# Clustered attention with a gated feed-forward layer on one core: one split and four loads moved in the listed opening, and a planner with other banks, dates and constants

## The chip, the cores and the metric

The kernel runs on one core of a Trainium2 chip. The time is the device time of one execution in microseconds (us), as the median of several runs. The engines are PE (TensorE, matrix products), ACT (ScalarE), DVE (VectorE), POOL (GpSimd) and SP, which here only issues DMAs. POOL issues DMAs too.

## What is computed

For 4 batches and 8 heads, queries and keys (768 tokens of 64 numbers) are each assigned to the nearest of 16 centroids of their head. A query attends only to keys of its own cluster. The result, 3072 tokens of 512 numbers, goes through `w_in` (512 to 2048), a SiLU gate and `w_out` (2048 to 512).

```python
    q_assign = np.argmax(np.einsum('bhsd,hcd->bhsc', q_n, c_n), axis=-1)
    k_assign = np.argmax(np.einsum('bhsd,hcd->bhsc', k_n, c_n), axis=-1)
    mask = q_assign[:, :, :, None] == k_assign[:, :, None, :]
    scores = scale * np.matmul(q, k.transpose(0, 1, 3, 2))
    scores = np.where(mask, scores, -1000000000.0)
    ...
    attn = attn / (np.sum(attn, axis=-1, keepdims=True) + 1e-09)
    return np.matmul(attn, v).astype(np.float32)
...
    h = x @ w_in
    g = h * (1.0 / (1.0 + np.exp(-h)))
    return (g @ w_out).astype(np.float32)
```

## The kernel before

**The work of one head.** A job holds the rows of q and k of one head and batch. Jobs 0 to 7 are batch 0 (`k0` to `k7`, with three of six query blocks; `x0` and `x1` hold the other three blocks of four heads each); jobs 8 to 31 are batches 1 to 3. A job's steps are:

- `load` (line 111, SP): the raw rows come in, as two DMAs for jobs 8 to 31 (q, then k).
- `hi` and `lo`: the rows are split into two f16 halves, upper and lower. The upper half is made by ACT, DVE or POOL (lines 123, 127, 125), the lower always by DVE (line 132), which reads the upper half.
- The halves are transposed into the tile `ab`: in batch 0 by PE (`tr`, line 155) and a copy out of the bank (`ev`, lines 164 and 166), in batches 1 to 3 by a DMA transpose that SP issues (`xpose`, line 141).
- Logits against the centroids on PE (`psN`, line 180, twelve small products), sums, maximum and comparison on DVE (lines 192, 208, 217). The codes of the cluster go into spare rows of `ab`: by a product with the identity, a copy (`cd`, line 257 or 259) and a small DMA (line 261), or in batches 2 and 3 by a DMA transpose (line 233) and a move from POOL (line 237). Two heads of batch 0 (`ct`) have no DMA in this.

**Units.** A unit is one pair of score products (`pS`, line 354) and one exponential on ACT (`P`, line 359). There are 192, 24 for each half of a batch, three for each head and half. The score tiles have two buffers. After six units, `pv` (line 371, 36 small products) makes the output of two heads, DVE normalises it, and it is transposed into `xt`.

**Feed-forward.** When four such pairs are done, sixteen pieces `a` (`ph`, line 421, four products with `win_s`) each give a gate (tanh on ACT, line 441, and product on DVE, line 444). Pieces `b` multiply by `wout_s`: plain tiles `po` in four quarters of four products (line 480), or pairs with seven products out of differences (line 562). Quarter n needs the four `w_out` chunks of piece n.

**Weights.** `w_in` comes in eight pieces (`w0` to `w7`, line 618) and `w_out` in four (`w8` to `w11`, line 621), all issued by POOL, which also casts values (`v`, line 295) and makes some upper halves. Their queue is apart from SP's. `w10` and `w11` wait for exponentials 22 and 23 by a small copy (line 614).

**Order.** Two things set it. The opening is the list `plan`, one word for each step, which writes each engine's instructions in that order: `hi6.P` is the upper half of job 6 on POOL, `lo6` its lower half, `tr6.20` its transposes into banks 2 and 0, `ce2.A` the copy of job 2's codes on ACT with the DMA behind it, `r8` the load of job 8, `e7.0` the end of piece `a` number 7 in bank 0. It ends with the eight gates `e0 e1 e6 e4 e2 e3 e5 e7`. Everything behind is written by a planner that keeps a clock for each engine and picks at each step a piece that is ready by its own costs and due times. Its constants: `PACE` and the like date the scores; `SPLIT` gives the unit at which a job of batches 1 to 3 is split, and `AHEAD`, `VALUES` and `CAST` how many units before or after it its rows, values and cast are asked for; `ROOM` (one for each of batches 1 to 3) is added to the time at which a transpose is taken to land, before the job's logits may be placed on PE; `CODES` and `TURN` do the same for codes and for `xt`; `MARGIN` decides when ACT takes a copy from DVE.

**Banks.** PE's small results share four banks. A piece of the planner takes the first bank of the list `free`, sorted by `freed`, the planned time of release. Before the change the planner starts with `free` as 0, 1, 2, 3, all with time 0.

Of the kernel before, what the change touches and what calls it, by code (L numbers as in the profile page):

```python
# [34 lines left out]
def kernel(  # L35
# [753 lines left out]
    plan = """  # L789
        hk0 hq0 hi1.A lk0 cn0 lq0 lo1 tk0.0 hi2.A evk0.D j3.1 c5.12 kad tq0.3 lo2 evq0.A tr1.23 stk vl4 L0.0 vl0  # L790
        evq1.A evk1.D mx0 ge0 hi4.A tr2.13 evq2.A L1.2 hi3.P ct0.03 lo4 mx1 ge1 xr0 cm1 ctk0 hi5.P evk2.A lo5 ctq0
        tr4.10 ce1.A qk0 hi7.P evk4.A lo3 L2.3 evq4.A tr5.21 mx2 evk5.D ge2 qk1 ex0 qk2 evq5.A w0 lo7 L4.0 vl1 ex1 mx4
        cm2 tr3.12 ex2 ce2.A xr1 qk3 evq3.D evk3.A qk4 hi6.P tr7.32 ge4 lo6 cm4 L3.1 evq7.D xh0.P ex3 qk5 vl2 evk7.D
        ce4.A v4 mx3 w1 ex4 tr6.20 evk6.D ex5 L5.3 ge3 mx5 vl5 qk6 v1 evq6.A ct3.21 vl3 ge5 qk7 cm5 L6.0 xl0 ctk3 ex6
        ctq3 qk8 ce5.A L7.S.2 xq0.3 mx6 ge6 w2 ls7 xp0.1 xw0.D v0 xh1.P ex7 cm6 v2 v5 qk9 ex8 ce6.A qk10 ex9 pa0.3 mx7
        ge7 pb0 vl6 xu0.D xl1 qk11 xL0.0 ex10 cm7 vl7 qk12 v3 ex11 xM0 ce7.D xs0 w3 pc0 v7 qk13 r8 xp1.1 ex12 qk14 xm0
        ex13 xu1.D ex14 w4 xq1.2 qk15 xg0 v6 nm0 pa1.1 qk16 xw1.D xc0 pt0.3 ex15 xe0.D ex16 qk17 ex17 xL1.2 w5 pb1
        qk18 vl8 ex18 xM1 qk19 pe0.D pc1 qk20 nm1 vl9 xs1 pa2.0 ex19 ex20 qk21 pb2 qk22 ex21 pc2 xm1 xg1 ex22 nm2 w6
        qk23 px3.3 pt1.1 pe1.D ex23 pt2.0 xc1 py3 qk24 pe2.D w7 r9 xe1.A r10 nm3 ex24 qk25 a0.1 pt3.0 w8 qk26 a1.2
# [559 lines left out]
```

## Time and profile before

| what | value |
|---|---|
| median of 3 runs | 299.75 us (299.74 to 303.74) |
| the profiled execution | 301.13 us |
| its span, first to last instruction | 298.7 us |
| PE busy | 288.7 us (97%) |
| DVE, ACT, POOL busy | 224.2, 217.8, 71.1 us |
| PE's waits for other engines and DMAs, all eight kinds | 6.3 us |

A profile's time is counted from the span's start. A row of a timeline gives start, length, engine, line, what is written and read, how many, and in brackets the idle time before and what ended it. A row on DMAs of a line gives their count, how long the issue took, when the first and last were issued, and below it the time from issue to landing (least, median, most).

### The profile page before, as it was taken

What the parts mean: (1) busy time and instruction counts of PE and PEld (TensorE: products, weight loads), DVE (VectorE), ACT (ScalarE), POOL (GpSimd) and SP (SyncE); (2) the same over time, 40 slices, a digit from 0 to 9 for tenths busy, and PEclk for the clock granted to TensorE, in tenths of its full rate; (3) what the DMA queues carried; (4) which work ended last, traced back from release to release, by engine and by line L of the source; (5) the groups of instructions that cost most, each with busy time, mean ns of one, the idle gap of its engine ahead of it and who ended that gap; (6) DMA issues with size and microseconds to landing.
All of it is one profiled execution on the core that took longest, in us unless ns stands there. A gap on an engine that the chain in (4) does not pass through costs nothing.

```text
span 298.7 us, 8186 instructions
## 1 busy us (share of the span) xinstructions
PE 288.7 (97%) x3281; PEld 204.1 (68%) x3281; DVE 224.2 (75%) x470; ACT 217.8 (73%) x357; POOL 71.1 (24%) x133
## 2 busy tenths in 40 slices
PE   7889989799999999999999999999999999999995
PEld 3777756466676566668766876678767777776884
DVE  5989678468999869999788966988674644469653
ACT  4989879653996569996488668997798788844410
POOL 2995710010042003453432214423200000000000
PEclk9999999999999999999999999999999999999999
DMA  6888999979999598999998699786400020110014
GB/s 210 248 199 161 191 250 214 160 200 206 226 215 230 117 181 200 256 182 214 180 194 165 136 180 262 178 137 114 115 22 15 13 87 13 50 37 0 35 37 140
DMA packets 77365, 44.61 MB, mean 149 GB/s; under 512 B 56305, under 2 KB 73233, under 8 KB 77329
## 3 DMA queue, kind: packets, MB, share of 16 engines
q1 hardware_dynamic: 72096, 35.62, 54.2%
q0 software_dynamic: 4800, 8.13, 14.9%
q8 instruction: 25, 0.41, 0.6%
q10 hardware_dynamic: 432, 0.36, 0.4%
q14 instruction: 12, 0.09, 0.1%
HBM read 27.30 MB, written 6.29 MB: 112 GB/s over the span
## 4 chain that ended last, share of the span: by engine, by line
PE 78%; DMA 11%; DVE 3%; ACT 3%; issue 2%; POOL 1%; SPq 1%; POOLq 0%; ACTq 0%; DVEq 0%
PE ph L421 24%; PE po L562 17%; PE pS L354 16%; PE pO L371 10%; DMA wout_s<-in_moe_w_out_dram 8%; PE po L480 7%; PE psN L180 3%; ACT P L359 2%; DMA ab<-cd 2%; DMA raw<-in_q_dram 1%; POOL hl L125 1%; DVE hl L132 1%; DVE ab L166 1%; DVE mxn L208 1%; SPq L111 0%
## 5 line engine op out<-in xcount | busy, mean ns | idle before, releaser
L359 ACT ACTIVATE P<-pS 128x768 f16<-128x768 f32 x192 | 156.3, 823 | 37.2 <-PE pS L354 36.5
L421 PE MATMUL ph<-xt,win_s 128*128 128x384 f16 x512 | 97.9, 326 | 0.8 <-DVE gt L444 0.8
L354 PE MATMUL pS<-ab 128*128 128x384 f16 x384 | 93.0, 326 | 0.5 <-DMA ab<-cd 0.3
L444 DVE SCALAR_TENSOR_TENSOR gt<-tn,ph 128x384 f16<-128x384 f32 x112 | 60.6, 550 | 21.4 <-ACT tn L441 20.6
L421 PEld LDWEIGHTS <-win_s 128*128 128x128 f16 x512 | 49.1, 98 | 31.9 <-issue 1.1
L441 ACT ACTIVATE tn<-ph 128x384 f32<-128x384 f32 x112 | 56.2, 507 | 5.9 <-PE ph L421 4.9
L354 PEld LDWEIGHTS <-ab 128*128 128x128 f16 x384 | 34.5, 98 | 19.0 <-DMA ab<-cd 0.9
L371 PEld LDWEIGHTS <-P 128*128 128x128 f16 x1152 | 39.9, 97 | 4.5 <-DVE ab L166 0.2
L371 PE MATMUL pO<-vt,P 128*128 128x65 f16 x1152 | 41.2, 193 | 0.0
L480 PE MATMUL po<-wout_s,gt 128*128 128x512 f16 x128 | 32.5, 379 | 1.8 <-DMA wout_s<-in_moe_w_out_dram 1.8
L132 DVE SCALAR_TENSOR_TENSOR hl<-raw,hl 128x768 f16<-128x768 f32 (+3 forms) x35 | 32.6, 938 | 1.6 <-POOL hl L125 1.0
L562 PEld LDWEIGHTS <-gt 128*128 128x128 f16 x312 | 29.4, 98 | 6.1 <-DVE gt L544 0.9
L295 POOL CAST vt<-vn 128x384 f16<-128x384 f32 x32 | 17.9, 562 | 52.3 <-DMA vn<-in_v_dram 46.5
L562 PE MATMUL po<-wout_s,gt 128*128 128x256 f16 x192 | 24.4, 273 | 0.1
L224 POOL TENSOR_SCALAR od<-od 128x96 f16<-128x96 f16 x16 | 8.3, 520 | 56.0 <-DVE od L217 55.9
L480 PEld LDWEIGHTS <-gt 128*128 128x128 f16 x128 | 12.2, 98 | 12.9 <-issue 2.0
L180 PEld LDWEIGHTS <-ab 128*128 128x128 f16 x458 | 17.4, 97 | 4.3 <-DVE ab L166 0.4
L383 DVE TENSOR_TENSOR xn<-pO,zr 128x384 f16<-128x384 f32 x32 | 17.8, 558 | 1.1
L180 PE MATMUL psN<-stk,ab 128*128 128x32 f16 (+1 forms) x458 | 18.6, 188 | 0.0
L192 DVE TENSOR_REDUCE L<-psN 128x192 f32<-128x384 f32 (+1 forms) x27 | 14.8, 549 | 2.9 <-PE psN L180 2.9
L381 DVE RECIPROCAL zr<-pO 128x6 f32<-128x6 f32 x32 | 6.2, 194 | 14.0 <-PE pO L371 13.6
L237 POOL DMA_DIRECT2D ab<-cdt x16 | 9.0, 565 | 31.6 <-PE pS L354 16.0
(101 smaller groups left out, 265.4 us busy)
## 6 DMA issues: line engine op xcount, KB each, us to landing
raw<-in_k_dram SPq DMA_DIRECT2D x31, 192.0 KB, 4.0
out_dram<-ot SPq DMA_DIRECT2D x23, 256.0 KB, 2.2
raw<-in_q_dram SPq DMA_DIRECT2D x24, 192.0 KB, 4.2
vn<-in_v_dram SPq DMA_DIRECT2D x16, 192.0 KB, 3.9
vn<-in_v_dram POOLq DMA_DIRECT2D x16, 192.0 KB, 3.9
win_s<-in_moe_w_in_dram POOLq DMA_DIRECT2D x8, 256.0 KB, 6.7
wout_s<-in_moe_w_out_dram POOLq DMA_DIRECT2D x4, 512.0 KB, 20.6
raw<-in_q_dram SPq DMA_DIRECT2D x2, 384.0 KB, 4.8
```

The lines of the kernel that those rows point to most:

```text
L132: nc.vector.scalar_tensor_tensor(out=hl[:, s, 1, :], in0=raws[job.name][:, s, :], scalar=QS, in1=hl[:, s, 0, :], op0=ALU.mult, op1=ALU.sub ...
L180: nc.tensor.matmul(L[:, n % g, :, n // g], ab[:, i, :], stk[:, job.groups[i // 3][0], x : x + w], start=(x == 0), stop=(x + w == 2 * HC),)
L295: nc.gpsimd.tensor_copy(vt[:, :, 0:D], vns.pop(i))
L354: nc.tensor.matmul(pS[:, e, 0:HALF], abs_[kj.name][:, kn, :], rhs, start=True, stop=True)
L359: nc.scalar.activation(out=P, in_=pst.pop(u)[:, :, 0:HALF], func=AF.Exp, bias=0.0, scale=ESC)
L371: nc.tensor.matmul(o[:, (2 * t + h) * VW : (2 * t + h + 1) * VW], Ps[i + h, c, j // 2][:, j % 2, ts(t, 128)], vtb[(i + h) % 13][:, j, 0:VW ...
L383: nc.vector.tensor_tensor(out=xn, in0=ov[:, :, 0:D], in1=zr.unsqueeze(2).to_broadcast([128, 2 * NM, D]), op=ALU.mult)
L421: nc.tensor.matmul(ph[:, 0:HALF], win_s[:, r, ts(fb, 128)], xts[b, c][:, r, :], start=(r == 0), stop=(r == NR - 1))
L441: nc.scalar.activation(out=tn, in_=ph[:, 0:HALF], func=AF.Tanh, bias=0.0, scale=1.0)
L444: nc.vector.scalar_tensor_tensor(out=gt[:, fb, :], in0=tn, scalar=1.0, in1=ph[:, 0:HALF], op0=ALU.add, op1=ALU.mult)
L480: nc.tensor.matmul(po, gts[b, c][:, fc, ts(t, 128)], wout_s[:, fc, :], start=(fc == 0), stop=(fc == NFB - 1))
L562: nc.tensor.matmul(o, l[:, f, :], x[:, x0 : x0 + w], start=(f == 0 and k in begins), stop=(f == HK - 1), skip_group_check=True)
```

## The change

In the list, `w0` and `w1` now stand together behind `hi6.P`, so that POOL makes the upper half of job 6 ahead of w_in's first piece; `w2` to `w7` each stand where the piece before them stood, and `w8` to `w11` stay. `r8` goes from behind `v7 qk13` to behind `vl1`, ahead of `ce2`. In the planner the banks start in the order 1, 2, 3, 0 with times of release of their own, a quarter of a plain tile gets a date for its piece of `w_out`, and most constants change.

```diff
-        evq1.A evk1.D mx0 ge0 ... evq5.A w0 lo7 L4.0 vl1 ex1 mx4
-        cm2 tr3.12 ex2 ce2.A xr1 qk3 evq3.D evk3.A qk4 hi6.P tr7.32 ...
+        ... evq5.A lo7 L4.0 vl1 r8 ex1 mx4
+        cm2 tr3.12 ex2 ce2.A xr1 qk3 evq3.D evk3.A qk4 hi6.P w0 w1 tr7.32 ...
...
-    freed = dict.fromkeys(range(4), 0.0)
+    free[:] = [1, 2, 3, 0]
+    freed = {1: -0.8, 2: -0.3, 3: 0.2, 0: 0.7}
     halls = []
-    free.append(3)
...
-    PACE, LEAST, LESS, GAIN = 1.4, 20, 20, 0.035
-    HOLD, ROUND, SIDE, LEAD = 10, 7, 4, 10
-    ROOM, CODES, TURN, BY_POOL = (0.8, 4.2, 5.0), 2.0, 0.5, 99
-    MARGIN = 1.1
-    EARLY_T = 62
+    PACE, LEAST, LESS, GAIN = 1.37, 23, 13, 0.03
+    HOLD, ROUND, SIDE, LEAD = -7, 8, 4, 11
+    WEIGHTS = 15.5
+    ROOM, CODES, TURN, BY_POOL = (1.3, 0.8, 2.0), 1.5, 1.0, 99
+    MARGIN = 0.1
+    EARLY_T = 67
...
-    moves_end = 13.2
+    moves_end = 12.0
...
-    SPLIT = [27, 27, 33, 34, 36, 47, 53, 55, 65, 70, ...]
-    AHEAD, VALUES, CAST = [11, 9, 18], [2, 4, 7], [6, 7, 7]
+    SPLIT = [27, 27, 33, 41, 43, 44, 51, 56, 67, 72, ...]
+    AHEAD, VALUES, CAST = [9, 8, 10], [1, 0, 4], [7, 3, 12]
...
-            need = [gate_at.get((b, c, fb)) for fb in range(4 * n, 4 * n + 4)] + ([bank_at] if n == 0 else [])
+            need = [WEIGHTS - (10.0, 7.4, 3.5, 0.0)[n]] + [gate_at.get((b, c, fb)) for fb in range(4 * n, 4 * n + 4)] + ([bank_at] if n == 0 else [])
```

On POOL, in the opening, the rows before and after are these (`hl_438` and `hl_440` are the halves of job 6, `hl_476` and `hl_480` those of `x0`, the numbers only count tiles):

```order
 L125 TENSOR_SCALAR hl_329<-raw_115 128x9x64
-L618 DMA win_s_66<-in_moe_w_in_dram 128x1024
-L125 TENSOR_SCALAR hl_438<-raw_112 128x9x64
-L125 TENSOR_SCALAR hl_476<-raw_300 128x12x64
+L125 TENSOR_SCALAR hl_440<-raw_112 128x9x64
+L618 DMA win_s_66<-in_moe_w_in_dram 128x1024 x2
+L125 TENSOR_SCALAR hl_480<-raw_300 128x12x64
 L295 CAST vt4_74<-vn_219 128x6x64
```

The split of job 6 goes ahead of the first piece of w_in, and the second piece now follows the first.

On SP, in the opening, these rows stand from the move of job 1's codes to that of job 4's before the change:

```order
L261 DMA ab_206<-cd_323 16x5x256
L290 DMA vn_403<-in_v_dram 128x384
L261 DMA ab_249<-cd_425 16x5x256
L113 DMA raw_428<-in_q_dram 128x4x192
L290 DMA vn_483<-in_v_dram 128x384
L261 DMA ab_311<-cd_486 16x5x256
```

and these after it (`raw_404` are the rows of job 8, `ab_249` takes job 2's codes):

```order
L261 DMA ab_206<-cd_323 16x5x256
L290 DMA vn_402<-in_v_dram 128x384
L111 DMA raw_404<-in_q_dram 128x384
L111 DMA raw_404<-in_k_dram 128x384
L261 DMA ab_249<-cd_427 16x5x256
L113 DMA raw_430<-in_q_dram 128x4x192
L290 DMA vn_487<-in_v_dram 128x384
L261 DMA ab_311<-cd_490 16x5x256
```

Two loads go ahead of the move of job 2's codes; before the change they stand further on in this queue.

On SP, where the planner begins, these rows stand before the change (`raw_1040` are the rows of job 11, `raw_1096` those of job 12, `ab_1128`, `ab_1268` and `ab_1428` the transposes of jobs 8, 9 and 10):

```order
L111 DMA raw_1040<-in_k_dram 128x384
L111 DMA raw_1096<-in_q_dram 128x384
L111 DMA raw_1096<-in_k_dram 128x384
L141 DMA_TRANSPOSE ab_1128<-hl_1099 128x12x128
L141 DMA_TRANSPOSE ab_1268<-hl_1103 128x12x128
L492 DMA out_0_dram<-ot_1355 128x512
L290 DMA vn_1368<-in_v_dram 128x384
L290 DMA vn_1409<-in_v_dram 128x384
L290 DMA vn_1416<-in_v_dram 128x384
L141 DMA_TRANSPOSE ab_1428<-hl_1214 128x12x128
```

and these after it (`raw_1354` are the rows of job 12, `raw_1369` those of job 13):

```order
L111 DMA raw_1040<-in_k_dram 128x384
L141 DMA_TRANSPOSE ab_1125<-hl_1096 128x12x128
L141 DMA_TRANSPOSE ab_1263<-hl_1100 128x12x128
L290 DMA vn_1326<-in_v_dram 128x384
L141 DMA_TRANSPOSE ab_1339<-hl_1211 128x12x128
L111 DMA raw_1354<-in_q_dram 128x384
L111 DMA raw_1354<-in_k_dram 128x384
L111 DMA raw_1369<-in_q_dram 128x384
L111 DMA raw_1369<-in_k_dram 128x384
L492 DMA out_0_dram<-ot_1388 128x512
```

The transposes of jobs 8, 9 and 10 go ahead of the rows of job 12, which now come together with those of job 13.

More of the change, by code (lines that the diff above doesn't have):

```diff
@@ L791 @@
         evq1.A evk1.D mx0 ge0 hi4.A tr2.13 evq2.A L1.2 hi3.P ct0.03 lo4 mx1 ge1 xr0 cm1 ctk0 hi5.P evk2.A lo5 ctq0
[L792 to L799, printed above, removed]
+        tr4.10 ce1.A qk0 hi7.P evk4.A lo3 L2.3 evq4.A tr5.21 mx2 evk5.D ge2 qk1 ex0 qk2 evq5.A lo7 L4.0 vl1 r8 ex1 mx4
+        cm2 tr3.12 ex2 ce2.A xr1 qk3 evq3.D evk3.A qk4 hi6.P w0 w1 tr7.32 ge4 lo6 cm4 L3.1 evq7.D xh0.P ex3 qk5 vl2 evk7.D
+        ce4.A v4 mx3 w2 ex4 tr6.20 evk6.D ex5 L5.3 ge3 mx5 vl5 qk6 v1 evq6.A ct3.21 vl3 ge5 qk7 cm5 L6.0 xl0 ctk3 ex6
+        ctq3 qk8 ce5.A L7.S.2 xq0.3 mx6 ge6 w3 ls7 xp0.1 xw0.D v0 xh1.P ex7 cm6 v2 v5 qk9 ex8 ce6.A qk10 ex9 pa0.3 mx7
+        ge7 pb0 vl6 xu0.D xl1 qk11 xL0.0 ex10 cm7 vl7 qk12 v3 ex11 xM0 ce7.D xs0 w4 pc0 v7 qk13 xp1.1 ex12 qk14 xm0
+        ex13 xu1.D ex14 w5 xq1.2 qk15 xg0 v6 nm0 pa1.1 qk16 xw1.D xc0 pt0.3 ex15 xe0.D ex16 qk17 ex17 xL1.2 w6 pb1
+        qk18 vl8 ex18 xM1 qk19 pe0.D pc1 qk20 nm1 vl9 xs1 pa2.0 ex19 ex20 qk21 pb2 qk22 ex21 pc2 xm1 xg1 ex22 nm2 w7
+        qk23 px3.3 pt1.1 pe1.D ex23 pt2.0 xc1 py3 qk24 pe2.D r9 xe1.A r10 nm3 ex24 qk25 a0.1 pt3.0 w8 qk26 a1.2
         pe3.D ex25 w9 e0 e1 w10 e6.3 r11 e4.0 ex26 e2.1 e3.2 e5.3 w11 e7.0
@@ L991, in cast @@
             add("POOL", max(t, values_at[i] + 0.4, pv_at[old] + 0.06 if i >= 13 else 0.0), 0.6, lambda: cast_v(i), done_)
-    SPLIT = [27, 27, 33, 34, 36, 47, 53, 55, 65, 70, 78, 79, 85, 87, 89, 95, 102, 109, 115, 121, 122, 132, 137, 142]
-    AHEAD, VALUES, CAST = [11, 9, 18], [2, 4, 7], [6, 7, 7]
+    SPLIT = [27, 27, 33, 41, 43, 44, 51, 56, 67, 72, 79, 80, 81, 83, 84, 87, 99, 102, 105, 122, 124, 132, 135, 142]
+    AHEAD, VALUES, CAST = [9, 8, 10], [1, 0, 4], [7, 3, 12]
     for i in range(H, B * H):
```

## The prediction

> **What bounds the kernel now.** I read the page's first part, then busy time by stage, then the list of who waited for whom on TensorE (PE). Here are the page's lines for the span and the engines, one stage behind 60 us (busy time of PE first, granted clock and DMA at the end), and the three of PE's waits that matter (total us, times, longest).
>
> ```profile
> span 298.7 us, 8186 instructions
> PE 288.7 (97%) x3281; PEld 204.1 (68%) x3281; DVE 224.2 (75%) x470; ACT 217.8 (73%) x357; POOL 71.1 (24%) x133
> ...
> 60.00:80.00 20.00, 20.00 (x230) 12.88 (x229) 15.81 (x35) 11.65 (x19) 2.03 (x4) 1.00 0.93 209
> ...
> PE po L480 <- DMA wout_s<-in_moe_w_out_dram: 1.8, 1, 1.8
> ...
> PE pTk L155 <- DVE ab L166: 0.8, 1, 0.8
> PE ph L421 <- DVE gt L444: 0.8, 1, 0.8
> ```
>
> PE is busy 97%, at a granted clock of 1.00, and once past 60 us it hardly waits. Work moved about there gains next to nothing and loses whatever new waits it makes. What can be won are waits ahead of 60 us: 1.8 (w_out), 0.8 (a copy, `ab` L166) and 0.8 (a gate, `gt` L444). On PE's timeline (start, length, idle before) they stand here, each with its predecessor.
>
> ```profile
> 17.16 0.48 PE L354 MATMUL pS<-ab 128*128 128x384 f16 x2
> 18.49 0.49 PE L155 MATMUL pTk<-ident,hl 128*128 128x128 f16 x6 [0.84 <-DVE ab L166]
> ...
> 19.49 0.48 PE L354 MATMUL pS<-ab 128*128 128x384 f16 x2
> ...
> 41.96 0.49 PE L354 MATMUL pS<-ab 128*128 128x384 f16 x2
> 43.29 0.81 PE L421 MATMUL ph<-xt,win_s 128*128 128x384 f16 x4 [0.84 <-DVE gt L444]
> ...
> 57.51 0.49 PE L354 MATMUL pS<-ab 128*128 128x384 f16 x2
> 59.80 1.02 PE L480 MATMUL po<-wout_s,gt 128*128 128x512 f16 x4 [1.81 <-DMA wout_s<-in_moe_w_out_dram]
> 60.66 0.49 PE L354 MATMUL pS<-ab 128*128 128x384 f16 x2
> 60.99 1.03 PE L480 MATMUL po<-wout_s,gt 128*128 128x512 f16 x4
> ```
>
> The last two rows give the pitch: after a pair of scores the next piece starts 0.33 us on (60.66 to 60.99). So each wait cost a little more than its idle: 18.49 - 17.16 - 0.33 = 1.0 us, 43.29 - 41.96 - 0.33 = 1.0 us, 59.80 - 57.51 - 0.33 = 1.96 us. PE's order is the same in both kernels up to the piece behind 60.99, so these can be compared place by place.
>
> **Split of job 6 ahead of w_in (POOL).** The rows are POOL's, then the vector engine's (DVE).
>
> ```profile
> 9.69 4.21 POOL L125 TENSOR_SCALAR hl<-raw 128x576 f16<-128x576 f32 x2
> 13.86 0.77 POOL L618 DMA_DIRECT2D win_s<-in_moe_w_in_dram  x1
> 14.66 2.10 POOL L125 TENSOR_SCALAR hl<-raw 128x576 f16<-128x576 f32 x1
> ...
> 12.32 1.22 DVE L132 SCALAR_TENSOR_TENSOR hl<-raw,hl 128x576 f16<-128x576 f32 x1
> 14.50 0.75 DVE L132 SCALAR_TENSOR_TENSOR hl<-raw,hl 128x576 f16<-128x576 f32 x1
> 15.76 0.32 DVE L217 TENSOR_TENSOR om<-psN,mxn 128x160 f16<-128x160 f32 x1
> 16.79 1.38 DVE L132 SCALAR_TENSOR_TENSOR hl<-raw,hl 128x576 f16<-128x576 f32 x1 [0.71 <-POOL hl L125]
> 18.09 0.34 DVE L166 COPY ab<-pTq 128x384 f16<-128x384 f16 x1
> ```
>
> POOL's split of job 6 (14.66) waits behind the issue of w_in's piece (13.86). DVE's lower half of job 6 (16.79) waits for it, the copy at 18.09 stands behind that on DVE, and PE (`tr6`) needs the bank that this copy empties at 18.49. Now the split starts at 13.9 and ends at 16.0. DVE is free at 16.08 (15.76 + 0.32), so 0.71 is won. Two durations are open. The lower half at 14.50 now falls beside the split: 0.75 as it was, or 1.22, as at 12.32 beside the split that ends at 13.90. Job 6's own half now runs while POOL only issues DMAs: 1.38 or 0.75. The good end wins 0.71 + 0.63, of which PE can use 1.0; the bad end wins 0.71 - 0.47 = 0.24. I take 0.6, the middle.
>
> [...]
>
> ScalarE's (ACT's) exponentials shift with PE. Behind it POOL issues one piece more ahead of batch 0's later casts, 0.6 us; DVE's wait for the next POOL split may become 0.3 us, which banks already free on PE cover; without them it would be 0.3 on PE.
>
> **Banks by release.** Before, the planner starts with banks 0, 1, 2, 3 in that order and takes bank 0, used by `e7`, the last of the eight listed gates; PE stood at 43.29 until it was done. Now bank 1 comes first (`e2`, fifth gate).
>
> ```profile
> 41.17 2.07 DVE L444 SCALAR_TENSOR_TENSOR gt<-tn,ph 128x384 f16<-128x384 f32 x4 [0.53 <-ACT tn L441]
> ```
>
> Its first quarter, `e2`, is done by about 41.7, before PE's 41.96 + 0.33. The whole 1.0 us goes. The gates behind are then late by up to that much, but four banks cover about four pieces; DVE's splits at 43 to 46 us stay in their places.
>
> **Batch 1's first rows early, and w_in moved up.** The next rows give issue times and, under each, the times to landing: w_in's last three pieces, w_out's last two, the first transpose of batch 1. Then two rows of the page (KB and median us to landing), a stage (GB/s last) and SP's row ahead of job 8's new place with the one that follows it.
>
> ```profile
> L618 POOL DMA_DIRECT2D win_s<-in_moe_w_in_dram x3: 527/535/547, 30.8 to 31.8; - x3
> DMA to landing us min/median/max: 9.0/10.4/11.5
> L621 POOL DMA_DIRECT2D wout_s<-in_moe_w_out_dram x2: 740/746/753, 34.6 to 35.6; - x2
> DMA to landing us min/median/max: 21.8/23.0/24.2
> L141 SPq DMA_TRANSPOSE ab<-hl x1: 5564/5564/5564, 45.1 to 45.1; - x1
> DMA to landing us min/median/max: 15.1/15.1/15.1
> ...
> raw<-in_k_dram SPq DMA_DIRECT2D x31, 192.0 KB, 4.0
> ab<-cd SPq DMA_DIRECT2D x6, 40.0 KB, 4.0
> ...
> 30.00:35.00 5.00, 4.78 (x95) 3.89 (x93) 2.99 (x8) 4.70 (x7) 4.47 (x9) 1.00 0.86 199
> ...
> 12.37 0.58 SPq L290 DMA_DIRECT2D vn<-in_v_dram  x1
> 15.49 0.59 SPq L261 DMA_DIRECT2D ab<-cd  x1
> ```
>
> From 30 us the transfers queue up. w_in's last piece lands at 31.8 + 11.5 = 43.3, the one before it (issued 0.5 earlier) at 31.3 + 10.4 = 41.7, w_out's last at 35.6 + 24.2 = 59.8, when PE's wait ends. w_in's later pieces each go one place forward on POOL, so that one piece fewer is queued: 43.3 - 41.7 = 1.6 us off w_out's landing. Job 8's two halves, 384 KB, leave the crowded stretch too. At 199 GB/s they are worth 1.9 us if w_out's queue gets all of that, and 0 if SP's other transfers do; I take 1.2, nearer to the upper end, since part of this queue stood alone with them around 30 us. So w_out lands at 59.8 - 1.6 - 1.2 = 57.0, between 56.3 and 58.2.
>
> What it costs: on SP job 8's two issues now stand between the last two rows. SP is free there from 13.0 to 15.5, so the move of job 2's codes is issued as before; but it may land later behind them. PE uses it at 19.49, now at 18.9. At the median of 4.0 it lands at 19.5, 0.6 too late. The other end is 0, since w_in's first piece no longer runs beside it. I take 0; PE's wait for w_out (below) would hide 0.8 of it.
>
> **The sum.** PE reaches the fourth quarter of the first output tile at 57.84 - 0.6 - 1.0 = 56.2 and waits for w_out until 57.0. It starts it 59.8 - 57.0 = 2.8 us earlier; the opening and bank terms are inside that, since w_out ends last.
>
> **Behind 60 us.** The constants reorder PE's pieces; their number stays 3281. Copies move from DVE to ACT (75% and 73% busy, so hidden by PE). The last product's tail is unchanged. On SP three transposes now precede job 12's rows. The first landed at 45.1 + 15.1 = 60.2; without job 12's 384 KB ahead of it (1.9 us) it should land at 58.3, and its logits are due at about 57.0 + 2 x (0.86 + 0.33) = 59.4 (two quarters, 60.66 - 59.80 each, and two pairs of scores). The planner's room for logits after a transpose (ROOM) grows by 0.5 us in batch 1 and falls by 4.2 - 0.8 = 3.4 in batch 2 and by 3.0 in batch 3. The dates for w_out (WEIGHTS) move no quarter ahead of 60 us, and are worth 0. The smallest and the largest of the eight gaps in batch 2 (issue, then logits), the second with its landing, show what that leaves:
>
> ```profile
> 115.11 1.41 SPq L141 DMA_TRANSPOSE ab<-hl  x1
> 124.53 0.51 PE L180 MATMUL psN<-stk,ab 128*128 128x32 f16 x12
> ...
> 129.34 1.99 SPq L141 DMA_TRANSPOSE ab<-hl  x1
> 140.24 0.51 PE L180 MATMUL psN<-stk,ab 128*128 128x32 f16 x12
> DMA to landing us min/median/max: 6.3/6.3/6.3
> ```
>
> 9.4 and 10.9 become 6.0 and 7.5, against 6.3 for this slow landing. One late by 0.3 or so is likely: I add 0.4, bounds 0 and 8 x 0.3 = 2.4. Net: 2.8 - 0.4 = 2.4 us. The profiled execution took 301.13 (span 298.7 and 2.4 around it); it is 1.4 above the median of 299.75, from which I subtract: 297.4.
>
> **The rivals.**
> - Transfers keep w_out back. Job 8's share goes to SP's other transfers and w_out lands at 58.2: 1.6 won, 0.4 lost, 298.6. The crowd on SP speaks for it, the empty stretch at 29.8 against. [...]
> - The change does not do what it says: the wait takes the place of those removed. If the three early transposes also eat the saved piece, w_out lands at 59.8 as before and the wait is 3.6: 299.75 + 0.4 = 300.2. Against it: fewer bytes are queued.
> - Slower: logits too early. In batch 2 the eight gaps average about 10.2, the middle of these two, and leave 6.8. It decides when the landing there averages 7.1, since 8 x 0.3 eats the gain; at 7.4 it is 8 x 0.6 = 4.8, and 299.75 - 2.8 + 4.8 = 301.8. Landings of 6.3 and a denser order speak for it; that PE's delay would also delay the next request speaks against.
>
> **Chances.** Forecast (296.2 to 298.1) 0.55, w_out kept back (298.6) 0.17, no gain (300.2) 0.12, logits early (301.8 and up) 0.13, something better than 296.2 0.03. The range 296.0 to 300.8 leaves out about 0.15. A measurement of this kernel tells about 2% (6 us) from no change. Faster by over that would need all of PE's idle, 0.01; slower needs twice the price of early logits, 0.04; within, 0.95.
>
> **What would show it.** Right: no idle at the `tr6` copy and at the ninth `ph`; w_out's last wait under 1 us; first logits without a wait. Wrong: `ab<-cd` ahead of a score near 19 us, `psN` L180 on PE's list of waits with several us, or `raw` late for DVE's split near 63 us.

## The result, and the profile after

The kernel after takes 303.61 us (median of 20 runs, 300.62 to 305.45); the kernel before, in the same series, 301.12 us (20 runs, 299.5 to 306.27). The ratio is 1.0069 with a 95% interval of 1.0045 to 1.0093 (it compares the means of the undisturbed executions, so it is not the ratio of the medians): slower by 0.7%, where a gain of 2.4 us had been forecast (297.4 us, range 296.0 to 300.8). In this longer series the kernel before itself is 1.4 us slower than the 299.75 us from which the forecast was counted; so the loss of 0.7% is to be set against the gain of 2.4 us, and not 303.61 against 297.4. The profiled execution of the kernel after took 303.66 us with a span of 301.9, so 3.2 us more span than before (298.7).

The page's first lines of the kernel after, the stage behind 60 us (PE's busy time first), and PE's list of waits (us in total, times, longest):

```profile
span 301.9 us, 8206 instructions
PE 290.9 (96%) x3281; PEld 205.8 (68%) x3281; DVE 219.1 (73%) x460; ACT 222.0 (74%) x365; POOL 74.4 (25%) x133
...
60.00:80.00 20.00, 20.00 (x230) 12.62 (x228) 14.59 (x31) 13.03 (x21) 2.99 (x4) 1.00 1.03 218
...
PE pS L354 <- DMA ab<-cd: 3.3, 1, 3.3
PE pS L354 <- DMA ab<-cdt: 1.6, 2, 1.4
```

The three waits that the prediction wanted to remove (w_out 1.8, the copy 0.8, the gate 0.8) are gone. Two others have come: scores that wait for the move of codes, `ab<-cd` in batch 0 and `ab<-cdt` in batch 2. Besides, PE is busy 2.2 us longer with the same 3281 products. PE's timeline shows the places (start, length, idle before), first the scores of head 2 of batch 0 and what follows, then the ninth `ph`, then the quarters of output tiles, then batch 2:

```profile
17.38 0.49 PE L354 MATMUL pS<-ab 128*128 128x384 f16 x2
17.70 0.50 PE L155 MATMUL pTk<-ident,hl 128*128 128x128 f16 x6
...
18.21 0.65 PE L180 MATMUL psN<-stk,ab 128*128 128x16 f16 x20
22.12 0.82 PE L354 MATMUL pS<-ab 128*128 128x384 f16 x2 [3.26 <-DMA ab<-cd]
...
27.76 0.81 PE L354 MATMUL pS<-ab 128*128 128x384 f16 x4
...
46.70 0.49 PE L354 MATMUL pS<-ab 128*128 128x384 f16 x2
47.03 0.81 PE L421 MATMUL ph<-xt,win_s 128*128 128x384 f16 x4
...
61.57 1.03 PE L480 MATMUL po<-wout_s,gt 128*128 128x512 f16 x4
62.43 0.49 PE L354 MATMUL pS<-ab 128*128 128x384 f16 x2
62.76 1.03 PE L480 MATMUL po<-wout_s,gt 128*128 128x512 f16 x4
...
166.08 0.50 PE L354 MATMUL pS<-ab 128*128 128x384 f16 x2 [0.25 <-DMA ab<-cdt]
171.81 0.50 PE L354 MATMUL pS<-ab 128*128 128x384 f16 x2 [1.39 <-DMA ab<-cdt]
```

The same place before, where the four scores of 27.76 stood:

```profile
22.87 0.88 PE L354 MATMUL pS<-ab 128*128 128x384 f16 x4
```

Up to 60 us PE's pieces are of the same kinds in the same order in both kernels, so the places can be set against each other. `tr6` starts at 17.70 instead of 18.49: 0.79 won. The next scores start at 22.12 instead of 19.49: now 2.63 behind. From there to the four scores it takes 5.64 us (22.12 to 27.76) instead of 3.38 (19.49 to 22.87): another 2.26 lost, 4.89 behind in all. At the scores ahead of the ninth `ph` it is 46.70 - 41.96 = 4.74, and at the `ph` itself 47.03 - 43.29 = 3.74, so the gate's wait gave back 1.00. At the place of w_out's wait it is 61.57 - 59.80 = 1.77: 1.97 given back. The waits for `ab<-cdt` add 1.64, which makes 3.4, against the 3.2 that the spans differ.

The 2.26 us are the clock (e4 below shows it: the same pieces in 3.40 us at full clock). The windows have length, busy time of PE, PEld, DVE, ACT and POOL with counts, then PE's granted clock, the DMA share and GB/s; first before, in one row, then after:

```profile
20.00:28.00 8.00, 7.95 (x144) 6.32 (x145) 7.76 (x20) 7.86 (x13) 6.25 (x8) 1.00 0.88 185
```

```profile
20.00:22.00 2.00, 0.00 (x0) 0.00 (x0) 0.47 (x1) 0.00 (x0) 1.81 (x4) 0.67 0.98 234
22.00:24.00 2.00, 1.88 (x12) 1.05 (x13) 0.00 (x0) 1.00 (x2) 0.11 (x1) 0.50 1.11 325
24.00:26.00 2.00, 2.00 (x28) 1.36 (x28) 1.04 (x4) 1.27 (x3) 2.00 (x2) 0.50 1.11 226
26.00:28.00 2.00, 2.00 (x27) 1.94 (x26) 1.36 (x4) 0.99 (x2) 0.98 (x3) 0.62 0.46 92
```

While PE stood still (18.86 to 22.12) its clock fell to half and stayed there: (1 - 0.67) x 2 / 0.5 = 1.32 us of half clock in the first window, 4 in the next two, (1 - 0.62) x 2 / 0.5 = 1.52 in the last, 6.84 us together. Of these 1.44 us still fall into the idle time (20.68 to 22.12). From 22.12 on PE is busy all the time, and it makes 67 products up to 28.00.

Why the codes were late is seen on the queues. For one line and stretch, the rows give the issues and, below, the time to landing. First w_in's pieces (L618) and the move of job 2's codes (L261) before, then after:

```profile
L618 POOL DMA_DIRECT2D win_s<-in_moe_w_in_dram x1: 773/773/773, 13.9 to 13.9; - x1
DMA to landing us min/median/max: 4.3/4.3/4.3
...
L261 SPq DMA_DIRECT2D ab<-cd x1: 593/593/593, 15.5 to 15.5; - x1
DMA to landing us min/median/max: 2.8/2.8/2.8
```

```profile
L618 POOL DMA_DIRECT2D win_s<-in_moe_w_in_dram x2: 558/670/782, 15.1 to 15.8; - x2
DMA to landing us min/median/max: 4.5/5.3/6.0
...
L261 SPq DMA_DIRECT2D ab<-cd x1: 587/587/587, 16.0 to 16.0; - x1
DMA to landing us min/median/max: 6.1/6.1/6.1
```

Before, w_in's piece lands at 13.9 + 4.3 = 18.2 and the move at 15.5 + 2.8 = 18.3. After, the second piece lands at 15.8 + 6.0 = 21.8 and the move at 16.0 + 6.1 = 22.1. The move, 40 KB, lands in both just behind the piece of w_in that was issued ahead of it on another queue.

### The profile page after: what moved, and what is told of

It is laid out like the page before. It is cut to its first block, busy times and chain, and to the rows that moved or that the text cites. A ratio compares the mean times of both kernels' runs of the same rounds, so it can differ in the third digit from the quotient of the medians.

```text
span 301.9 us, 8206 instructions
## 1 busy us (share of the span) xinstructions
PE 290.9 (96%) x3281; PEld 205.8 (68%) x3281; DVE 219.1 (73%) x460; ACT 222.0 (74%) x365; POOL 74.4 (25%) x133
## 4 chain that ended last, share of the span: by engine, by line
PE 87%; DMA 6%; ACT 3%; SPq 1%; issue 1%; POOL 1%; DVE 0%; POOLq 0%; ACTq 0%
PE ph L421 27%; PE pS L354 19%; PE po L562 16%; PE pO L371 11%; PE po L480 9%; PE psN L180 3%; DMA ab<-cdt 3%; ACT P L359 2%; DMA ab<-cd 2%; DMA raw<-in_q_dram 1%; SPq L111 1%; POOL hl L125 1%; PE px L393 1%; DVE hl L132 0%; PE pC L268 0%
## 5 line engine op out<-in xcount | busy, mean ns | idle before, releaser
L354 PE MATMUL pS<-ab 128*128 128x384 f16 x384 | 94.0, 329 | 5.2 <-DMA ab<-cd 3.3
L444 DVE SCALAR_TENSOR_TENSOR gt<-tn,ph 128x384 f16<-128x384 f32 x110 | 58.7, 550 | 21.5 <-ACT tn L441 20.9
L441 ACT ACTIVATE tn<-ph 128x384 f32<-128x384 f32 x110 | 55.4, 516 | 3.2 <-PE ph L421 2.3
L354 PEld LDWEIGHTS <-ab 128*128 128x128 f16 x384 | 34.6, 98 | 24.1 <-DMA ab<-cd 3.4
L295 POOL CAST vt<-vn 128x384 f16<-128x384 f32 x32 | 19.8, 626 | 55.7 <-DMA vn<-in_v_dram 50.9
L562 PEld LDWEIGHTS <-gt 128*128 128x128 f16 x312 | 29.5, 98 | 5.9 <-DVE gt L544 0.4
L132 DVE SCALAR_TENSOR_TENSOR hl<-raw,hl 128x768 f16<-128x768 f32 (+3 forms) x35 | 31.9, 917 | 0.9 <-ACT hl L123 0.3
L224 POOL TENSOR_SCALAR od<-od 128x96 f16<-128x96 f16 x16 | 9.0, 566 | 55.5 <-DVE od L217 55.4
L192 DVE TENSOR_REDUCE L<-psN 128x192 f32<-128x384 f32 (+1 forms) x27 | 14.8, 549 | 4.0 <-PE psN L180 3.8
L562 PE MATMUL po<-tw,sg 128*128 128x256 f16 x128 | 16.3, 273 | 0.0
```

What stands on the lines that cost most here:

```text
L132: nc.vector.scalar_tensor_tensor(out=hl[:, s, 1, :], in0=raws[job.name][:, s, :], scalar=QS, in1=hl[:, s, 0, :], op0=ALU.mult, op1=ALU.sub ...
L295: nc.gpsimd.tensor_copy(vt[:, :, 0:D], vns.pop(i))
L354: nc.tensor.matmul(pS[:, e, 0:HALF], abs_[kj.name][:, kn, :], rhs, start=True, stop=True)
L441: nc.scalar.activation(out=tn, in_=ph[:, 0:HALF], func=AF.Tanh, bias=0.0, scale=1.0)
L444: nc.vector.scalar_tensor_tensor(out=gt[:, fb, :], in0=tn, scalar=1.0, in1=ph[:, 0:HALF], op0=ALU.add, op1=ALU.mult)
L562: nc.tensor.matmul(o, l[:, f, :], x[:, x0 : x0 + w], start=(f == 0 and k in begins), stop=(f == HK - 1), skip_group_check=True)
```

## The experiments

Each kernel's edit is against the kernel after, unless it says otherwise; "old list" is the `plan` of before. Two things are measured: the ratio to the kernel before, timed on the same chip, and the profile. Since the half clock comes in some executions of a kernel and not in others, the mean granted clock of each timed execution is used too. In the profiles it is 0.998 or more where no such stretch occurs besides the last microseconds (before 1.0, e13 0.999; those last microseconds, 298 to 302, have a clock of 0.82 in the kernel after), 0.992 to 0.994 with one (e2, e9, e8), and 0.987 or 0.988 with two (after, e10, e11). All timed executions lie at 0.997 or more, at 0.992 to 0.994, or at 0.987 to 0.989.

### One half of the change taken back

Theory A in the first four expectations puts the late move down to w_in's pieces, theory B to the rows of job 8.

```diff
 e1: -  evq5.A lo7 L4.0 vl1 r8 ex1 mx4 ... v7 qk13 xp1.1
     +  evq5.A lo7 L4.0 vl1 ex1 mx4 ... v7 qk13 r8 xp1.1
 e2: -  hi6.P w0 w1 tr7.32 ... mx3 w2 ... ge6 w3 ... (w4 to w7)
     +  hi6.P w0 tr7.32 ... mx3 w1 ... ge6 w2 ... (w3 to w7 as before)
 e3:    the old list, with the planner of after
 e4: -  vl5 qk6 v1
     +  vl5 j15.2 qk6 v1        (15 products by zero that nothing reads)
```

The rows of job 8 late again:

> The changed kernel with the load of job 8 alone back at its old place in the list (behind the values of head 7). In the changed kernel PE waits 3.3 us near 19 us for the codes of job 2, whose move was issued at 16.0 and took 6.1 us, and the granted clock is 0.5 to 0.67 from 20 to 28 us. Theory A (the two w_in pieces issued together at 15.05 and 15.8, just ahead of the move, hold it): the wait stays, 2 to 3.5 us, the low clock too, and the ratio to before stays at 1.003 to 1.009. Theory B (job 8's rows, ahead of the move on SP's queue, hold it): the wait is under 0.7 us, the clock 1.0, and 4 to 5 us come back, ratio 0.988 to 0.994.

Measured: 302.87 us, ratio 1.001 (0.997 to 1.0054), between the ranges of the two theories; the wait is 3.21 us, as in the kernel after and as A says. With two pieces of w_in ahead of it, the rows of job 8 are not what makes the move late.

Only one piece of w_in behind the split of job 6:

> The changed kernel with w_in's second to eighth piece back at their old places, so that the split of job 6 is still ahead of the first piece, but only one piece is issued ahead of job 2's move; job 8's rows stay early. Theory A (two pieces together hold the move): the wait is under 0.7 us, the clock 1.0, and 4 to 5 us come back: ratio 0.988 to 0.994. Theory B (job 8's rows): the wait of 2 to 3.5 us stays, ratio 1.003 to 1.009. w_out's last piece should land 1 to 2 us later against its issue than in the changed kernel, and PE may wait for it by as much.

Measured: 301.86 us, ratio 0.9997 (0.996 to 1.004); the move takes 5.3 us, the wait is 2.49, this time as B says, with a ratio again between the ranges. One piece makes PE wait nearly as long as two, as long as the rows of job 8 are early.

The whole list of before:

> The list of before with the planner of after (banks, dates, constants). Both theories: no wait for job 2's codes; the 0.8 us wait ahead of the transposes of job 6 is back; the 0.8 us wait for a gate is gone (banks). If the early pieces of w_in and job 8's rows are what moved w_out, PE waits for w_out again, by 2 to 3 us near 57 us; if not, that wait is under 1 us. The waits for moved codes near 166 to 172 us (1.6 us in the changed kernel) stay if the planner makes them. Ratio 0.998 to 1.006.

Measured: 299.64 us, ratio 0.987 (0.980 to 0.994); the move takes 2.5 us, no wait at head 2, none for w_out and none for the gate's bank. So the list alone carries the loss, and the planner's part is a gain. The expectation was wrong in the ratio (0.998 to 1.006), and the wait of 0.8 us ahead of `tr6`, which it had coming back, didn't come.

PE kept busy while it waits:

> The changed kernel with 15 idle-time products on zeros (not part of the computation) on PE ahead of the first scores of head 2, where it waits. If the low clock from 20 to 28 us follows from PE's idle stretch, it stays at 1.0, the stretch from the first scores of head 2 to the ninth pair takes 3.4 us instead of 5.6, and the time falls by 2 to 2.5 us: ratio 0.997 to 1.002. If the clock is lowered by something else, it is low all the same and the time stays or grows: ratio 1.005 to 1.01.

Measured: 302.13 us, ratio 0.9997 (0.9965 to 1.003). The move lands later still (6.7 us), and yet PE's clock stays full. The first two rows are the scores of head 2 and the four scores:

```profile
22.82 0.50 PE L354 MATMUL pS<-ab 128*128 128x384 f16 x2 [0.20 <-DMA ab<-cd]
...
26.22 0.88 PE L354 MATMUL pS<-ab 128*128 128x384 f16 x4
...
20.00:22.00 2.00, 2.00 (x11) 0.88 (x9) 0.84 (x1) 0.00 (x0) 1.19 (x2) 1.00 1.03 199
22.00:24.00 2.00, 1.80 (x15) 0.85 (x14) 0.00 (x0) 0.65 (x1) 0.00 (x0) 1.00 1.13 336
```

From one to the other it is 3.40 us, against 5.64 in the kernel after and 3.38 before, so the 2.26 us are gone. All ten timed executions have a mean clock of 0.998 or more, against 19 of 20 below 0.996 in the kernel after. So the half clock is a consequence of the idle time, not of the moves.

### Which part of the list

Theory C: the move is held by the piece of w_in issued shortly ahead of it. Rival D: by the sum of what is asked for, job 8's rows among it.

```diff
 e5: -  hi6.P w0 w1 tr7.32 ... evq7.D xh0.P ex3
     +  hi6.P tr7.32 ... evq7.D xh0.P w0 w1 ex3
 e6 (old list):  -  evq5.A w0 lo7 ... hi6.P tr7.32
                 +  evq5.A lo7 ... hi6.P w0 tr7.32
 e7 (old list):  -  vl1 ex1 mx4 ... v7 qk13 r8 xp1.1
                 +  vl1 r8 ex1 mx4 ... v7 qk13 xp1.1
 e8 (before):    -  freed = dict.fromkeys(range(4), 0.0)
                 -  free.append(3)
                 +  free[:] = [1, 2, 3, 0]
                 +  freed = {1: -0.8, 2: -0.3, 3: 0.2, 0: 0.7}
```

w_in's two pieces one split later:

> The kernel after, in which POOL asks for w_in's first two pieces one split later, behind the 12 head split of batch 1's rows (xh0, 2.67 us) and so some 2.7 us later, near 17.7 us; the split of job 6 keeps its early place. Theory C (a w_in piece asked for just ahead of the move of job 2's codes, which SP issues at about 16 us, slows that move from 2.8 to 6.1 us): the move lands in 2.5 to 3.5 us again, scores of head 2 start by 19.5 us, the wait of 3.3 us for ab<-cd is gone, the granted clock stays near 1.0 between 20 and 28 us, and the ratio to the kernel before is 0.983 to 0.992. Rival D (the move is slow because of all that SP itself asks for between 13 and 18.5 us, rows of batch 1 among it): the move still takes 5 us or more, the wait stays over 2 us and the ratio is 0.998 to 1.008.

Measured: 302.08 us, ratio 1.0026 (1.0 to 1.005). C's mechanism holds for the move in question, 2.4 us and no wait at head 2; its time doesn't. The next two moves, issued behind the pieces, are late in its place, as their landing and PE show:

```profile
L261 SPq DMA_DIRECT2D ab<-cd x2: 562/564/567, 21.9 to 23.9; - x2
DMA to landing us min/median/max: 7.5/7.5/7.6
...
29.55 0.50 PE L354 MATMUL pS<-ab 128*128 128x384 f16 x2 [1.72 <-DMA ab<-cd]
```

The first lands at 21.9 + 7.6 = 29.5, when PE goes on. Eight of ten executions show a half clock (mean below 0.996).

The swap with w_in's first piece alone:

> The list of before with one edit, w_in's first piece (w0) behind the split of job 6 instead of ahead of it; no other piece moves, batch 1's rows stay late; the planner behind the list is that of after. It is compared with the old list in the same planner, which took 0.987 of the time before. Theory C: w0 is now issued at 15 to 16 us, the move of job 2's codes takes 5 us or more, PE waits 2 to 3.3 us for ab<-cd near 21 us, the granted clock falls to 0.5 to 0.7 behind it, and the ratio is 0.994 to 1.004, 2 to 5 us over the old list. Rival D (only together with the rows of batch 1 asked for early): the move takes 2.5 to 3.5 us and the ratio is 0.984 to 0.990.

Measured: 300.07 us, ratio 0.994 (0.990 to 0.998); one of ten executions with a half clock. C's numbers were too large: piece and move went out together (15.48 and 15.51), the move took 4.3 us, and PE waited a little:

```profile
19.82 0.50 PE L354 MATMUL pS<-ab 128*128 128x384 f16 x2 [0.37 <-DMA ab<-cd]
```

The rows of job 8 alone:

> The list of before with one edit, the rows of batch 1's first job (r8) asked for early, at their place in the kernel after; all pieces of w_in stay at their old places; the planner is that of after. Theory C: the early rows cost nothing, the move of job 2's codes takes 2.5 to 3.5 us, the wait for ab<-cd stays under 1 us, ratio 0.984 to 0.990. Rival D: the move takes 4.5 us or more, a wait over 1.5 us near 21 us, and a ratio of 0.993 to 1.003.

Measured: 299.42 us, ratio 0.9925 (0.990 to 0.995), no half clock in four executions. The move took 4.0 us and PE waited between the two forecasts:

```profile
20.26 0.50 PE L354 MATMUL pS<-ab 128*128 128x384 f16 x2 [1.17 <-DMA ab<-cd]
```

The ratio, too, lies between them. Swap and rows each cost little alone; e2, which has both, waits 2.49. Neither C nor D says this as stated; what is common is put together below.

The banks alone:

> The kernel before with one edit, the planner starts with the four banks in the order in which the list frees them (1, 2, 3, 0, with their dates) and no bank is put in twice; list and constants are those of before, so that every engine has the same instructions in the same order and only banks differ. The prediction's term for this was 1.0 us (a wait of 0.84 us for the gate's bank near 43.3 us, with what lies around it). If the term holds: that wait is gone and the ratio is 0.995 to 0.998. Rival: it returns at the next bank, a wait of 0.5 us or more for another reader between 43 and 60 us, and the ratio is 0.999 to 1.002.

Measured: 300.39 us, ratio 0.9965 (0.993 to 0.9997): 1.05 us at 301.5 (0.1 to 2.0 by the interval), as the prediction's term says. The gate's wait is gone; a wait of 0.61 us for w_in came near it, and the one for w_out stays at 1.98. This profile is of the one execution of the ten with a stretch of half clock (304.17 us); it begins behind the wait for w_out.

### Order, dose and kind

```diff
 e9:  -  evq5.A lo7 ... hi6.P w0 w1 tr7.32
      +  evq5.A w0 w1 lo7 ... hi6.P tr7.32
 e10 (rows of job 8 late, as in e1):
      -  hi6.P w0 w1 tr7.32 ... mx3 w2 ex4
      +  hi6.P w0 w1 w2 tr7.32 ... mx3 ex4
 e11: the list of after, with the planner of before
 e13 (from e5):
      -  vl1 r8 ex1 ... pe2.D r9 xe1.A
      +  vl1 r8 r9 ex1 ... pe2.D xe1.A
```

Two pieces ahead of the split:

> The kernel after with one edit: POOL asks for w_in's first two pieces together ahead of the split of job 6, near 13.5 us, where before asks for the first one; batch 1's rows stay early, every other engine has the instructions of after. In the profiles so far the move of job 2's codes landed no more than 0.5 us after the last piece of w_in that was issued ahead of it wherever that piece landed at 20 us or later, and 0.1 to 1.5 us after it where the piece was issued by 13.9 us. Theory C (the piece issued just ahead of the move holds it): pieces issued at 13.5 and 14.2 us land by 19.5 us, the move by 20 us; the wait for ab<-cd near 20 us is 0.3 to 1.5 us instead of 3.3, the granted clock has no half speed block in most executions, and the ratio is 0.986 to 0.996. Rival D (the sum of all that is asked for between 12 and 16 us decides, 1088 KB as in the kernel after, whatever its order): the move lands past 21 us, the wait is over 2.5 us, the clock is halved in most executions, and the ratio is 0.999 to 1.008.

Measured: 302.71 us, ratio 1.003 (0.9996 to 1.006), all ten executions with a half clock, a wait of 2.35 us. An earlier place doesn't help two pieces: issued at 14.0 and 14.8 beside the rows of job 8, the second lands at 14.8 + 7.2 = 22.0, and the move at 22.2. C's condition (issued by 13.9) was wrong: the move followed the second piece's landing (22.0), not the place of its issue. And where the expectation gives 1.5 us as the longest way from a piece's landing to the move's, e7 has 2.2 (18.0 to 20.2).

Three pieces behind it:

> The kernel with batch 1's rows back at their late place, and three pieces of w_in (768 KB) together behind the split of job 6 where the run with two (512 KB) had a move of 6.1 us and the run with one (256 KB) a move of 4.3 us. Theory C: the move of job 2's codes lands when the third piece does, 7.5 to 9 us after its issue at 16.5 us, PE waits 4.5 to 6 us for ab<-cd near 24 us, the clock is halved for two blocks or more, and the time is 303 to 307 us. Rival D (SP's own requests decide): the move takes about 6 us as with two pieces, a wait of 3 to 3.5 us, 301 to 303 us.

Measured: one execution, 305.28 us. The wait and the move's landing:

```profile
23.97 0.82 PE L354 MATMUL pS<-ab 128*128 128x384 f16 x2 [4.78 <-DMA ab<-cd]
...
DMA to landing us min/median/max: 7.6/7.6/7.6
```

A third piece adds 1.5 us to the move and 1.6 to the wait, as C says and D doesn't.

The list in the planner of before:

> The list of after with the planner of before: its banks, dates and constants. It completes the square of list and planner (old list with the new planner took 0.987 of the time before, new list with new planner 1.007). If the list is what loses, whatever stands behind it: the wait of 3.2 us for ab<-cd near 22 us and the halved clock are there, and the ratio is 1.005 to 1.025 (the list's own loss of about 2 per cent, less what the wait for w_out, 1.8 us, gives back). If instead list and planner do harm only together, the ratio is 0.993 to 1.003.

Measured: 307.62 us, ratio 1.020 (1.012 to 1.028), a wait of 4.60 us at head 2 and half clock in all four executions. The list loses in either planner.

The same bytes as rows on SP's own queue:

> The run with w_in's pieces behind the split of x0 (no piece of w_in ahead of the move of job 2's codes, 384 KB of rows ahead of it, a move of 2.4 us) with one edit: the rows of job 9 are asked for right behind those of job 8, so that 768 KB of rows stand ahead of the move in SP's own queue within 3 us, as much as three pieces of w_in. If bytes in flight ahead of the move decide, whatever their queue: the move lands only when the last rows have, 5 to 7.5 us after its issue, PE waits over 1.5 us near 21 us. If w_in's pieces (POOL's queue, with a change of type) are what holds it: the move takes 2.4 to 3.8 us and the wait near 20 us stays under 0.7 us.

Measured: one execution, 301.17 us. The rows (four loads of 192 KB) and below them the move:

```profile
L111 SPq DMA_DIRECT2D raw<-in_q_dram x2: 359/386/413, 14.0 to 15.0; - x2
L111 SPq DMA_DIRECT2D raw<-in_k_dram x2: 430/430/430, 14.5 to 15.4; - x2
DMA to landing us min/median/max: 2.5/3.7/3.9
...
L261 SPq DMA_DIRECT2D ab<-cd x1: 587/587/587, 16.2 to 16.2; - x1
DMA to landing us min/median/max: 3.3/3.3/3.3
```

768 KB of rows ahead of the move leave it at 3.3 us; 768 KB of w_in (e10) make it 7.6. And 384 KB of rows on top of two pieces delay it by no more than 0.1 us (e1, landing at 22.0, and after, at 22.1). So a piece of w_in holds the move much more than rows do. Two things limit this. The bytes are the same only where they are written: w_in comes as f32 and is stored as f16, so that a piece of 256 KB reads 512 KB. The page of the kernel after agrees with it, since the inputs in f32 are 18.9 MB for q, k and v and 8.4 MB for the two weights:

```profile
HBM read 27.30 MB, written 6.29 MB: 111 GB/s over the span
```

So e10's pieces read 1536 KB, and the bytes read are not ruled out as what makes them slow. And the rows of e13 land by 15.4 + 3.9 = 19.3, the move 0.2 behind them: here too the move lands with what was issued ahead of it, only the rows land sooner. A later move, at 29.80, is late by 2.34 us in e13, much as in e5.

The profiles, by when the last piece of w_in issued ahead of the move, or within 0.1 us of it, lands:

| run | w_in ahead, issued at | last lands | move issued, lands | PE's wait |
|---|---|---|---|---|
| e5 | none | - | 16.1, 18.5 | 0 |
| e13 | none | - | 16.2, 19.5 | 0.45 |
| e3 | 13.3 | 18.0 | 16.0, 18.5 | 0 |
| before | 13.9 | 18.2 | 15.5, 18.3 | 0 |
| e7 | 13.5 | 18.0 | 16.2, 20.2 | 1.17 |
| e6 | 15.5 | 20.3 | 15.5, 19.8 | 0.37 |
| e2 | 15.2 | 21.3 | 16.2, 21.5 | 2.49 |
| e1 | 14.9, 15.7 | 21.7 | 15.9, 22.0 | 3.21 |
| after | 15.1, 15.8 | 21.8 | 16.0, 22.1 | 3.26 |
| e9 | 14.0, 14.8 | 22.0 | 15.9, 22.2 | 2.35 |
| e4 | 14.9, 15.7 | 22.4 | 16.1, 22.8 | 0.2, after the added products |
| e11 | 15.2, 16.0 | 23.3 | 16.1, 23.6 | 4.60 |
| e10 | 15.1, 15.8, 16.4 | 24.1 | 16.3, 23.9 | 4.78 |

Where w_in lands at 20 us or later, the move lands from 0.5 us ahead of it to 0.4 behind it. Where it lands by 18.2 or nothing of it is ahead, the move takes 2.4 to 4.0 us, the longest behind the rows of job 8 (e7). In e8, e12 and e14, which have the old list, the piece lands by 17.7 and the move takes 2.4 to 2.6 us. One piece lands 4.3 to 4.8 us after its issue where the rows of job 8 are late or come behind it (before, e3, e6, e7); with these rows ahead of it 6.1 (e2), and a second piece 6.0 to 7.3. That is how the parts add up: swap and rows together, or two pieces, push the landing behind 21 us, where PE has nothing left to do.

### The planner's part

The old list in the new planner, once more:

> The same kernel as in the run with the old list and the new planner, measured again in more rounds, since its first interval was wide (0.980 to 0.994). If the planner part alone is a gain of banks by release and no more (the run with the banks alone took 0.9965), the ratio is 0.994 to 0.999. If the dates and constants give as much again, it is 0.985 to 0.994, with no wait for ab<-cd over 1.2 us, none for w_out and none for the gate's bank in the profile, and a granted clock of 0.998 or more in nearly all executions.

Measured: 299.45 us, ratio 0.991 (0.987 to 0.995), no execution below a clock of 0.997. PE's longest wait for `ab<-cd` is 1.23 us, at 28.08; there is none for w_out or for the gate's bank. It is faster than both kernels: 0.991 stands against 1.0069 for the kernel after.

Dates for w_out beside the banks (against e8):

```diff
+    WEIGHTS = 15.5
...
-            need = [gate_at.get((b, c, fb)) ...
+            need = [WEIGHTS - (10.0, 7.4, 3.5, 0.0)[n]] + [gate_at.get((b, c, fb)) ...
```

> The kernel before with the banks by release and, new against the run with the banks alone, the dates for w_out; the list and all other constants are those of before. The dates put the first quarter of the second output tile ahead of the last quarter of the first, as in the kernel after. If the dates are what removes the wait for w_out in the old list: the last quarter starts one place (1.2 us) later, the wait there falls from 1.98 us to 0.8 or less, and the ratio is 0.990 to 0.995 (banks alone 0.9965). If the wait goes only by transfers that land earlier: it stays over 1.2 us at the later place and the ratio is 0.995 to 1.000. What the other pieces of the plan do behind 63 us, where the order changes too, can move either by some tenths of a per cent.

Measured: 302.14 us, ratio 1.002 (0.998 to 1.007). The wait falls as forecast:

```profile
59.26 1.02 PE L480 MATMUL po<-wout_s,gt 128*128 128x512 f16 x4 [0.38 <-DMA wout_s<-in_moe_w_out_dram]
```

The last of w_out lands at 35.6 + 23.7 = 59.3, in e8 at 35.3 + 24.2 = 59.5: the later place does it, not an earlier landing. The time lies above both forecasts, if by less than its interval: the plan behind 63 us changed too, and PE has new waits of 1.6 us for exponentials there, near 108 and 181 us. So the dates remove the wait for w_out; that the other constants are needed to keep the gain is argued from e3 and e12, not shown one by one.

## Why the prediction was wrong

- **The step that failed** is the cost of the queue: "The other end is 0, since w_in's first piece no longer runs beside it. I take 0". It looked only at the place that the piece left, and not at the one that it went to. Before, the piece had landed by 18.2, in time for a move needed at 19.49; the change put two pieces right ahead of the move, and it landed at 22.1. The bounds of 0 to 0.6 us came from the median move (4.0 us) in the whole page, and the landing of w_in's pieces was never set beside that of the move. By the prediction's own dates the two pieces would have gone out at the end of the split, at 16.0, half a microsecond behind the move (15.5), and so beside it. In the run the split ended at 15.10 and the move went out at 16.0, so that they went ahead of it. Measured: 3.26 us of idle time.
- **A term that wasn't in the sum** is the clock. The row of 1.00 in the profile of before held only as long as PE had no gap of this size; 2.26 us more. The two are the result: the old list in the same planner has neither and takes 299.5 us (e3, e12).
- **Split of job 6** (0.6 us, bounds 0.24 to 1.0): 0.79 at `tr6`; the whole wait went, and PE stood 0.22 later ahead of it (17.38 instead of 17.16). The lower half of job 7 beside POOL's split took the good end, and job 6's own half came in between:

```profile
14.56 0.74 DVE L132 SCALAR_TENSOR_TENSOR hl<-raw,hl 128x576 f16<-128x576 f32 x1
...
16.05 1.04 DVE L132 SCALAR_TENSOR_TENSOR hl<-raw,hl 128x576 f16<-128x576 f32 x1
```

  POOL's splits ran until 15.10; the first of these started at 14.56 beside them and took 0.74 us, as long as in the kernel before (0.75). But the gain was spent at once on a longer wait at the next scores, and e7 has no wait at `tr6` with w_in's piece still ahead of the split, so the wait of before wasn't firm either.
- **Banks** (1.0 us): 1.00 by the places, 1.05 by e8. Right.
- **w_out** (2.8 us at its quarter, with a landing at 57.0): the wait is gone, but not by that. The last of w_out lands later than before:

```profile
L621 POOL DMA_DIRECT2D wout_s<-in_moe_w_out_dram x4: 740/766/787, 37.7 to 40.3; - x4
DMA to landing us min/median/max: 12.6/16.6/20.4
```

  At 40.3 + 20.4 = 60.7, against 59.8. Its issues wait for exponentials, so the late opening made them late, and PE was later still. And "The dates for w_out (WEIGHTS) move no quarter ahead of 60 us, and are worth 0" was wrong. Written with the tiles' numbers, the first product behind a pair of scores at the place of the old wait is, before and after:

```
1416 L480 MATMUL po_1261<-wout_s_67,gt_1021 128x512
1416 L480 MATMUL po_1344<-wout_s_67,gt_1021 128x512
```

  `po_1261` is the first output tile of before, `po_1344` the second of after: the last quarter of the first tile now comes one place later (62.76). Read without numbers, the two orders are alike, and the prediction took them for the same. With the old list (e3) this and an earlier landing (35.7 + 22.0 = 57.7, used at 58.10) remove the wait; there the term would have come out nearly as forecast, for another reason.
- **Behind 60 us** (0.4 us, bounds 0 and 2.4, through logits): 1.64 us, through codes (`ab<-cdt`). No logits were late in the kernel after. These waits differ from run to run, 0 in before, e3, e7 and e14, 0.5 to 2.2 in the others, and 0 and 0.9 in two profiles of the same kernel (e3 and e12); what sets them was not settled.
- **The rivals.** The slower one, logits too early, didn't come. In the other two w_out lands at 58.2 or 59.8; it landed later than that, at 60.7, and cost nothing, since its use had moved to 62.76. What did make the kernel slower, `ab<-cd` ahead of a score near 19 us, was among the signs to look for, but had no price above 0.6 us and no chance of its own.

## What to carry to other kernels

A small transfer that PE needs must be dated by when the big ones issued ahead of it land, on its own queue (e13: rows at 19.3, move at 19.5) or on another (e10: last piece at 24.1, move at 23.9); set issue and landing of both side by side before a load is moved across it. An early load that is not needed early is best left where its landing falls ahead of the small one (before: 18.2 and 18.3, with no wait at head 2). And an idle time of PE can have a second price in clock: in these profiles waits of 2.0 to 2.5 us brought a stretch of half clock in three cases (1.4 and 1.65 us more in the two worked out below) and none in e13 (2.34 us), and the wait of 3.26 us cost 2.26 us more.

## What the runs showed of the hardware

**The half clock came in stretches of 3.4 and 6.84 us.** In e2, with 2.49 us of idle time ending at 21.57, the windows are:

```profile
22.00:24.00 2.00, 2.00 (x35) 1.64 (x35) 0.63 (x2) 1.65 (x3) 1.19 (x1) 0.68 1.09 234
24.00:26.00 2.00, 2.00 (x27) 1.66 (x24) 1.15 (x4) 1.62 (x3) 1.39 (x2) 0.50 1.06 244
26.00:28.00 2.00, 2.00 (x37) 1.67 (x36) 1.97 (x5) 1.36 (x3) 0.77 (x2) 0.97 0.14 38
```

By the same working as above this is 1.28 + 2 + 0.12 = 3.4 us of half clock, half of the 6.84 in the kernel after, and it begins 1.1 us after PE went on. From these scores to the four scores PE takes 4.82 us (21.57 to 26.39), against 3.40 in e4, so it cost 1.4 us. In e8 one cost 1.65: 59.57 to 64.69 for the pieces that take 59.80 to 63.27 before.

How much idle time brings it, the profiles show only in part. Waits of 1.98 (e8, ahead of w_out), 2.35 (e9) and 2.49 us (e2) each went with one such stretch (mean clock 0.994, 0.993 and 0.992), those of 3.26 (after), 4.60 (e11) and 4.78 us (e10) with two (0.987, 0.988 and 0.988). The 1.81 us in the profile of before went with none (1.0), and neither did the 2.34 us of e13 (0.999). e1 has a wait of 2.21 us beside that of 3.21, and a mean clock of 0.989, as with two stretches for both together. The rows are those of e1 and e13, and the last is the window behind that of e13:

```profile
172.08 0.50 PE L354 MATMUL pS<-ab 128*128 128x384 f16 x2 [2.21 <-DMA ab<-cdt]
...
29.80 0.50 PE L354 MATMUL pS<-ab 128*128 128x384 f16 x2 [2.34 <-DMA ab<-cd]
...
30.00:32.00 2.00, 2.00 (x40) 1.65 (x38) 0.68 (x2) 1.66 (x3) 0.21 (x1) 1.00 0.84 158
```

Why 2.34 us cost nothing in e13 where 1.98 did in e8, and why executions of one kernel differ, was not shown.

**The small move landed with the pieces of another queue.** The move has 40 KB, a piece of w_in 256 KB as written. In the table above the move lands no more than 0.5 us ahead of the last piece (e6) where the pieces land at 20 us or later, though they stand on POOL's queue and it on SP's: in the kernel after it takes 6.1 us behind two of them and lands at 22.1, they by 21.8. In e13 it lands with the rows on its own queue, which land sooner (3.3 us behind 768 KB, at 19.5 against 19.3). Why the pieces take so much longer than the rows was not tried: the queue, the change of type and the bytes read all differ.
